# Reordered sums on VectorE and a full-width state decay in a retention plus maxout-FFN kernel

## The chip, the cores and the metric

The kernel runs on one core of one Trainium2 chip. The metric is the device time of one execution in microseconds. Four runs of the kernel before gave 776.54, 776.88, 778.55 and 776.59 us, a median of 776.73 us. The profile was taken on one execution, and its times are read with the clock of that execution; the granted TensorE clock was 1.00 over the whole span.

## The reference

```python
# q, k, v: (8, 8, 576, 64); x: 4608 tokens of 512
scores = scale * np.matmul(q, k.transpose(0, 1, 3, 2))
gamma = 1.0 - 2.0 ** (-5.0 - np.arange(H))
Dmat = np.where(rel >= 0, gamma ** rel, 0.0)          # rel = position of query - position of key
attn_out = np.matmul(scores * Dmat, v)
x = attn_out.transpose(0, 2, 1, 3).reshape(B * S, H * D)
h = np.maximum(np.maximum(x @ w1, x @ w2), x @ w3)    # 512 -> 768
out = h @ w_out                                       # 768 -> 512
```

The weights w1, w2, w3 and w_out arrive as float64 and are converted on the chip; everything is computed in float32.

## The kernel before

**Tiles and stages.** The 4608 tokens are 36 chunks of 128 (C) and 9 tiles of 512 (NT), numbered t = 0 to 8. Attention goes chunk by chunk with a running state: `scores` makes the products of queries and keys, `state` and `keep` carry the sum of keys times values to the next chunk, `values` makes the attention output, which is the FFN's input xT. `keep` multiplies a state by the decay over one chunk, gs, on VectorE (a chunk that starts a sequence, line 268) or on GpSimd (line 271). The FFN of tile t runs on TensorE (PE) while the attention of tile t + 1 is threaded into it: the last loop of the kernel alternates the steps that `steps(t + 1)` lists with `next(work)` on the generator `ffn(t)`. So the order on every engine is written out by hand; no scheduler moves anything.

**Plain and summed products.** A plain up product multiplies 512 tokens by one of w1, w2, w3 for one block of 128 hidden columns (`up_plain`, PE line 610); the first of the three is copied to h by ScalarE (line 615) and the other two are joined into h by a maximum on VectorE (line 614). Tile t = 0 does all its blocks in that way, and tile t = 1 the blocks fb = 2 and 3. Every other block uses `up`: a scheme with 20 smaller products in place of 24, whose factors are sums of pieces of x (X_SUMS) and of the weights (W_SUMS), and whose outputs are joined by VectorE additions and maxima (line 567, JOINS) after ScalarE copied them out of PSUM (line 572). The down product is plain for t = 0 (`downs_plain`, line 597) and a seven-product scheme after it (`downs`, line 427).

**The sums.** X_SUMS are 13 additions or subtractions of 128x256 on VectorE for each tile t > 0. W_SUMS are 19 such operations for each pair fp of hidden blocks, done once, in place where possible. All of them are issued by `combine`, line 346. They are queued in the list order: `weight_sums(0)` and `weight_sums(2)` at the start of tile t = 1, `weight_sums(1)` after its plain blocks. The sums for w_out (`sums_of_outs`, two on VectorE, lines 386 and 387, and two on GpSimd, lines 390 and 391, for each of three pairs) are queued while tile t = 0 does its down products.

**Who issues them and when.** `chore(n)` takes n entries from two queues, `urgent` first (attention work of VectorE that `soon` put off) and then `chores` (the sums). In tile t = 0 the down loop calls `chore(2)` after each of fb = 3, 4 and 5. In tile t = 1 each plain block has three steps, one for each of w1, w2, w3; a step issues its PE products and its copy or maximum, and after it `chore(8)` is called:

```python
for step, cost in enumerate(steps_of_one):
    if fb in plain:
        chore(8)
```

So the entries that `chore` issues after the step of w2 stand on VectorE's queue ahead of the maximum of w3.

**PSUM.** Plain and summed products share two pools of two banks each: ps_x (plain block 2, then chains A and B of the summed products) and ps_y (plain block 3, then chains E, C and D). A bank is handed out again when its last reader, a ScalarE copy or a VectorE operation, is done. After the plain block 3 of tile t = 1, chain E takes the bank that the maximum of w2 read, and chain C the one that the maximum of w3 reads.

**The start.** SyncE (SP) issues the loads: q, k and v of chunk 0 and of chunk 1, then the two loads of gs (line 692), then those of chunks 2 and 3 with the first weights between them. gs is 128 rows by 4 head pairs by 1 number; its source in HBM has 64 equal numbers for each head and row, of which one is read. The tile named fill only takes room.

Of the kernel before, what the change touches and what calls it, by code (L numbers as in the profile page):

```python
# [40 lines left out]
FP32 = mybir.dt.float32  # L41
# [4 lines left out]
ALU = mybir.AluOpType  # L46
# [4 lines left out]
NH = NT // 2  # L51
BY_PE = 7
AHEAD = 3
FILL = 192
PARTS = 20

X_SUMS = """s19 = a12 + a14, s15 = s19 - a22, s3 = a22 - a12, s10 = s3 - a13, s13 = a12 + a13, s20 = s10 + a23,
            s14 = a24 - s15, s11 = s20 + a24, s11 = a21 - s11, s7 = s11 - s13, s6 = s19 + s7,
            s16 = a11 - s11, s16 = s16 - a14"""
W_SUMS = """b33 = b13 + b33, n1 = b13 + b43, n2 = n1 - b41, n3 = b11 - n2, n4 = b33 - b32, b43 = b43 + n4,  # L60
            b23 = b43 - b23, b43 = b41 - b43, n5 = b22 + b23, b41 = b41 - n5, b21 = b21 - b41,
            b23 = b32 + b23, b22 = b22 - b21, b32 = b22 - b32, n6 = b31 + n2, n7 = b42 + n4,
            b42 = b42 - n5, b31 = b31 + b32, n8 = b12 - n4"""

PRODUCTS = """E a11 b12, E a14 b42, B s15 n5, A a22 b21, C s3 b23, B s19 b41, A s10 b32, C a13 b31, B s6 n2, A s13 b22,
              C a11 b11, B s14 n1, A s11 n4, D s7 b43, B a23 n6, A s20 b33, D s16 b13, B a21 n3, A a21 n8, A a24 n7"""
# [6 lines left out]
         "A7": [("A1", ("A1", "B6"), ALU.add), ("A1", ("A1", "A5"), ALU.max), ("hi", ("A1", "A7"), ALU.max)]}  # L73
X_SUMS, W_SUMS = ([x.split() for x in text.split(",")] for text in (X_SUMS, W_SUMS))
PRODUCTS = [x.split() for x in PRODUCTS.split(",")]
# [4 lines left out]
def kernel(  # L80
# [14 lines left out]
    nc = tc.nc  # L95
    P = 128
    B, H, S, D = q.shape
    N, DM = out.shape
    DF = moe_w1.shape[1]
    NP = H // 2  # L100
# [6 lines left out]
    const = ctx.enter_context(tc.tile_pool(name="const", bufs=1))  # L107
# [18 lines left out]

    gk = const.tile([C, H], FP32, name="gk")
    one, top, inf, first = (const.tile([P, 1], FP32, name=n) for n in ("one", "top", "inf", "first"))
    gs = const.tile([P, NP, 1], FP32, name="gs")
    const.tile([P, FILL // 4], FP32, name="fill")  # L130
    gq = const.tile([P, 2, NP // 2, C], FP32, name="gq")
    nc.scalar.dma_start(gk[:], key_decay)
    nc.vector.memset(one[:], 1.0)
    nc.scalar.copy(first[:], one[:])
# [15 lines left out]
    def start_of(g):  # L150
        r = -g * C % S
        return r if r < C else None
# [21 lines left out]
    def chore(n=1):  # L174
        for _ in range(n):
            if urgent or chores:
                (urgent or chores).popleft()()  # L177

    def soon(step):

        if spread:
            urgent.append(step)
        else:
            step()
# [63 lines left out]
    def begins(g):  # L248
        return g + 1 < NG and start_of(g + 1) != 0

    def half(j):
        return slice(D * j, D * (j + 1))
# [12 lines left out]
    def keep(g):  # L265
        def step(t, kv):
            if start_of(g) is not None:
                nc.vector.tensor_tensor(t[:], kv[:], gs[:].to_broadcast([P, NP, D]), op=ALU.mult)
            else:
                nc.vector.tensor_tensor(t[:], kv[:], states[g][:], op=ALU.add)  # L270
                nc.gpsimd.tensor_tensor(t[:], t[:], gs[:].to_broadcast([P, NP, D]), op=ALU.mult)

        if begins(g):
            t = states[g + 1] = stp.tile([P, NP, D], FP32, tag="state", name="state")
            soon(partial(step, t, kvs[g]))
# [46 lines left out]
    def output(chunks, o, t, i):  # L322
# [9 lines left out]
        if i == CPT - 1 and t > 0:  # L332
# [4 lines left out]
            def step(n, dst, _, a, sign, b):  # L337
                combine(*(xS[t][x] for x in (dst, a, b)), sign)
                if dst not in (later[0] for later in X_SUMS[n + 1:]):
                    made[t].add(dst)  # L340

            for n, line in enumerate(X_SUMS):
                soon(partial(step, n, *line))

    def combine(dst, a, b, sign):
        nc.vector.tensor_tensor(dst, a, b, op=ALU.add if sign == "+" else ALU.subtract)  # L346
# [191 lines left out]
    def weight_sums(fp):  # L538
# [3 lines left out]

        for dst, _, a, sign, b in W_SUMS:
            chores.append(partial(step, dst, a, sign, b))
        chores.append(partial(summed_fp.add, fp))

    def late_room():
        pool = late["pool"]
        late["W"] = [pool.tile([P, NF, P], FP32, name=f"n{n}") for n in range(1, 9)]
        late["X"] = {n: pool.tile([P, NH], FP32, name=n)[:] for n in sorted({x[0] for x in X_SUMS})}  # L550

    converting = convert_all()

    def convert(n):
        for _ in range(n):
            next(converting, None)
# [35 lines left out]
    def downs_plain(t, h):  # L592

        ps = [(ps_x, ps_y)[m % 2].tile([P, DM], FP32, tag="xy"[m % 2], name="down") for m in range(NT // P)]
        for fb in range(NF):
            for m, b in enumerate(ps):
                nc.tensor.matmul(b[:], lhsT=h[:, fb, m * P:(m + 1) * P], rhs=w_sb["out", fb],  # L597
                                 start=(fb == 0), stop=(fb == NF - 1))
                if fb == NF - 1:
                    osb = opool.tile([P, DM], FP32, tag="osb", name="osb")  # L600
                    nc.scalar.copy(osb[:], b[:])
                    nc.sync.dma_start(out[t * NT + m * P:t * NT + (m + 1) * P, :], osb[:])
            yield

    def up_plain(t, h, fb, i):
        ps = (ps_x, ps_y)[fb % 2].tile([P, NT], FP32, tag="xy"[fb % 2], name="up")
        first_of_all = t == 0 and (fb, i) == (0, 0)
        for cols in (slice(0, NT - C), slice(NT - C, NT)) if first_of_all else (slice(0, NT),):
            for dc in range(NDC):
                nc.tensor.matmul(ps[:, cols], lhsT=w_sb[i, fb][:, dc * P:(dc + 1) * P], rhs=xT[t][:, dc, cols],  # L610
                                 start=dc == 0 and cols.start == 0, stop=dc == NDC - 1,
                                 skip_group_check=first_of_all)
        if i > 0:
            return lambda: nc.vector.tensor_tensor(h[:, fb, :], h[:, fb, :], ps[:], op=ALU.max)
        return lambda: nc.scalar.copy(h[:, fb, :], ps[:])

    def ffn(t):

        h = hpool.tile([P, NF, NT], FP32, tag="h", name="h")
        if t == 0:  # L620
            for fp, i in units:
                for fb in (2 * fp, 2 * fp + 1):
                    maximum = up_plain(t, h, fb, i)
                    if CPT not in qks:
                        maximum()
                        transposes(CPT)
                        convert(4)
                        continue
                    convert(4)
                    maximum()  # L630
                yield
            convert(6)
            for fb, _ in enumerate(downs_plain(t, h)):
                convert(4 if fb < 2 else 4 * len(pieces))
                if fb == 2:
                    while_converting.close()
                    late["pool"] = ctx.enter_context(tc.tile_pool(name="late", bufs=1))
                    late_room()
                    sums_of_outs()
                elif fb > 2:  # L640
                    chore(2)
                if fb in (1, 3):
                    yield
            yield
            return
        if t == 1:
            spread.append(True)
            weight_sums(0)
            weight_sums(2)
        plain = (2, 3) if t == 1 else ()  # L650
        order = (2, 3, 0, 1, 4, 5) if t == 1 else (0, 1, 4, 5, 2, 3)
        total = sum(24 if fb in plain else len(PRODUCTS) for fb in order)
        count = parts = 0
        for n, fb in enumerate(order):
            if fb not in plain:
                while fb // 2 not in summed_fp:
                    chore()
            steps_of_one = up_plain_all(t, h, fb) if fb in plain else up(t, h, fb)
            for step, cost in enumerate(steps_of_one):
                if fb in plain:  # L660
                    chore(8)
                elif step % 2 or step % 5 == 4:
                    chore(len(urgent) > 0)
                elif step % 4 == 2 and chores:
                    chores.popleft()()
                count += cost or 1
                if count * (NF // 2 * 3) >= (parts + 1) * total:
                    parts += 1
                    yield
            if n % 2:  # L670
                sums_of_hidden(h, fb // 2)
                if fb in plain:
                    weight_sums(fb // 2)
        chore(len(urgent))
        for n, _ in enumerate(downs(t, h)):
            chore(4)
            if n in (1, 3):
                yield
        yield
# [8 lines left out]
    for g in range(CPT):  # L688
        load(g)
        if g == 1:  # L690
            for j in range(2):
                nc.sync.dma_start(gs[half(j)], state_decay[half(j), :, D * j:D * j + 1])
    load_weights(1)
    load(CPT)
    load_weights(4)
# [131 lines left out]
```

## Time and profile before

| what | value |
|---|---|
| median of 4 runs | 776.73 us |
| the profiled execution, its own time | 776.54 us |
| its span, first to last instruction | 774.8 us |
| PE busy | 766.9 us (99%) |
| VectorE (DVE) busy | 566.6 us (73%), 1249 instructions |
| ScalarE (ACT) busy | 326.1 us (42%) |
| GpSimd (POOL) busy | 99.2 us (13%) |
| DMA, first 20 us | 0.98 of 16 engines, 224 GB/s |
| DMA, 160 to 180 us | 0.39 of 16 engines, 74 GB/s |

The span lacks 1.74 us of the execution's own time; that part lies outside the instructions. A busy PE is not proof that it never waits, because the ends of pipelined matmuls are modelled; where it waits is read from the times at which matmuls start, and from the list of waits. Times "at 148.29" are microseconds from the start of the span. A timeline row gives start, duration, engine, line, operation, written and read tiles with their shape, the count, and in brackets idle time ahead of it and what ended it.

### The profile page before, as it was taken

Reading aid. Unit: us, or ns where it says so; the run is one execution under the profiler, and the core shown is the slowest. Engines: PE = TensorE matmul, PEld = TensorE weight load, DVE = VectorE, ACT = ScalarE, POOL = GpSimd, SP = SyncE. Lnnn points to the kernel's source line nnn. Section 1 sums busy time; section 2 is a strip of 40 time slices with the busy share of each in tenths; the row PEclk is TensorE's granted clock in tenths of the full one; section 3 lists DMA queues with packets and bytes.
Section 4 is the critical chain, followed back from the end, with each engine's and each line's share of the span. In section 5 each row is a group of like instructions: output and inputs, shape, how many; then the busy total and the mean of one; then the engine's idle time right before and its main releaser. Section 6 shows DMA issues by size and latency. Waiting matters only on the chain.

```text
span 774.8 us, 14508 instructions
## 1 busy us (share of the span) xinstructions
PE 766.9 (99%) x5032; PEld 626.5 (81%) x5032; DVE 566.6 (73%) x1249; ACT 326.1 (42%) x811; POOL 99.2 (13%) x124
## 2 busy tenths in 40 slices
PE   9899999999999999999999999999999999999998
PEld 7545454688888888888888888888888888888887
DVE  3998979899677857785769657875778567855672
ACT  3665631154154514452345234532544154514651
POOL 2110012111101201111111111110012001200000
PEclk9999999999999999999999999999999999999999
DMA  9995643333333332343233333333333324001001
GB/s 224 240 224 130 169 102 100 57 58 60 87 58 58 58 75 54 61 81 67 61 55 58 58 97 59 57 58 96 58 56 58 80 48 81 2 15 41 2 1 55
DMA packets 237082, 59.20 MB, mean 76 GB/s; under 512 B 217936, under 2 KB 235728, under 8 KB 237008
## 3 DMA queue, kind: packets, MB, share of 16 engines
q1 hardware_dynamic: 236432, 57.94, 34.8%
q8 instruction: 39, 0.64, 0.3%
q10 hardware_dynamic: 576, 0.33, 0.1%
q14 instruction: 35, 0.29, 0.1%
HBM read 48.76 MB, written 9.44 MB: 75 GB/s over the span
## 4 chain that ended last, share of the span: by engine, by line
PE 94%; DVE 4%; DMA 1%; issue 0%; ACT 0%; POOL 0%; DVEq 0%; POOLq 0%; ACTq 0%
PE a L587 18%; PE b L587 15%; PE dx L427 11%; PE up L610 8%; PE c L587 8%; PE dz L427 5%; PE d L587 5%; PE e L587 5%; PE s L242 4%; PE o L298 4%; PE dy L427 3%; PE down L597 2%; PE kv L262 2%; PE o L311 2%; DVE w L346 1%; DVE n L346 1%
## 5 line engine op out<-in xcount | busy, mean ns | idle before, releaser
L567 DVE TENSOR_TENSOR part<-part 128x256 f32<-128x256 f32 x460 | 207.1, 459 | 80.6 <-ACT part L572 72.9
L572 ACT COPY part<-b 128x256 f32<-128x256 f32 x230 | 85.7, 372 | 125.7 <-PE b L587 112.5
L572 ACT COPY part<-a 128x256 f32<-128x256 f32 x276 | 102.8, 373 | 84.9 <-PE a L587 74.0
L610 PE MATMUL up<-xT,w 128*128 128x512 f32 (+2 forms) x200 | 84.7, 578 | 1.5 <-DVE w L516 1.5
L587 PE MATMUL a<-s,w 128*128 128x256 f32 x276 | 82.3, 380 | 0.0
L213 POOL TENSOR_TENSOR vd<-vraw,gk 128x512 f32<-128x512 f32 x36 | 40.1, 1113 | 328.9 <-DMA vraw<-in_v_dram 228.4
L587 PE MATMUL b<-s,n 128*128 128x256 f32 x276 | 82.1, 379 | 0.0
L610 PEld LDWEIGHTS up<-xT,w 128*128 128x128 f32 x200 | 36.8, 190 | 43.6 <-issue 39.2
L587 PEld LDWEIGHTS b<-s,n 128*128 128x128 f32 x276 | 52.4, 190 | 7.1
L587 PEld LDWEIGHTS a<-s,w 128*128 128x128 f32 x276 | 52.3, 190 | 7.3 <-issue 0.2
L587 PE MATMUL c<-xT,w 128*128 128x256 f32 x184 | 56.0, 386 | 0.0
L587 PE MATMUL b<-xT,n 128*128 128x256 f32 x184 | 55.3, 382 | 0.0
L587 PE MATMUL d<-s,w 128*128 128x256 f32 x184 | 54.7, 379 | 0.0
L587 PE MATMUL a<-xT,n 128*128 128x256 f32 x184 | 47.2, 379 | 0.0
L587 PE MATMUL e<-xT,w 128*128 128x256 f32 x184 | 47.2, 379 | 0.0
L567 DVE TENSOR_TENSOR h<-part 128x256 f32<-128x256 f32 x92 | 41.8, 455 | 6.6
L427 PE MATMUL dx<-To,H 128*128 128x256 f32 (+1 forms) x204 | 44.9, 370 | 0.0
L434 ACT COPY part<-dx 128x256 f32<-128x256 f32 (+1 forms) x34 | 10.5, 362 | 80.1 <-PE dx L427 77.9
L177 DVE TENSOR_TENSOR xT<-o,gq 128x512 f32<-128x512 f32 x28 | 18.1, 686 | 33.9 <-PE o L311 33.9
L427 PEld LDWEIGHTS dx<-To,H 128*128 128x128 f32 x204 | 36.6, 190 | 5.5 <-issue 1.0
L242 PEld LDWEIGHTS s<-qT,kT 64*128 64x128 f32 x576 | 33.8, 188 | 7.9 <-PE b L587 4.0
L587 PEld LDWEIGHTS e<-xT,w 128*128 128x128 f32 x184 | 35.0, 190 | 5.2 <-issue 0.2
(104 smaller groups left out, 1283.0 us busy)
## 6 DMA issues: line engine op xcount, KB each, us to landing
bits<-in_moe_w_dram SPq DMA_DIRECT2D x36, 256.0 KB, 5.0
out_dram<-osb SPq DMA_DIRECT2D x35, 256.0 KB, 2.1
kraw<-in_k_dram SPq DMA_DIRECT2D x32, 256.0 KB, 2.9
vraw<-in_v_dram SPq DMA_DIRECT2D x32, 256.0 KB, 3.5
qraw<-in_q_dram SPq DMA_DIRECT2D x464, 16.0 KB, 1.8
kxraw<-in_k_dram SPq DMA_DIRECT2D x464, 16.0 KB, 1.8
bits<-in_moe_w_out_dram SPq DMA_DIRECT2D x6, 512.0 KB, 4.6
qraw<-in_q_dram SPq DMA_DIRECT2D x6, 256.0 KB, 4.4
```

What stands on the lines that cost most here:

```text
L177: (urgent or chores).popleft()()
L213: nc.gpsimd.tensor_tensor(t[:], raws.pop(("v", g))[:], gk[:].unsqueeze(2).to_broadcast([C, H, D]), op=ALU.mult)
L242: nc.tensor.matmul(s[j][:, p, :], lhsT=kT[r, p, :], rhs=qT[r, p, :], start=True, stop=True)
L262: nc.tensor.matmul(kvs[g][half(h % 2), h // 2, :], lhsT=kr[r:, h, :], rhs=vds[g][r:, h, :], start=True, stop=True)
L298: nc.tensor.matmul(o[n % 2][half(c), m, n // 2, :], lhsT=vds[g][:, h, :], rhs=sts[g][:, h % 2, h // 2, :], start=m == 0 and n < 2, stop=be ...
L311: nc.tensor.matmul(o[n % 2][half(c), m, n // 2, :old], lhsT=states[g][r, h // 2, :], rhs=qks[g]["q"][r, h // 2, :old], start=False, stop=True,
L346: nc.vector.tensor_tensor(dst, a, b, op=ALU.add if sign == "+" else ALU.subtract)
L427: nc.tensor.matmul(o, lhsT=hS[n](fp)[:, m * P:(m + 1) * P], rhs=late["T"][n][:, fp, cols], start=first and fp == 0 and (m == 0 or last and ...
L567: nc.vector.tensor_tensor(out, a, b, op=op)
L572: nc.scalar.copy(t[:], ps[step[0]][:])
L587: nc.tensor.matmul(ps[chain][:], lhsT=factor(w, fb), rhs=xS[t][x], start=n == 1, stop=ends, skip_group_check=True)
L610: nc.tensor.matmul(ps[:, cols], lhsT=w_sb[i, fb][:, dc * P:(dc + 1) * P], rhs=xT[t][:, dc, cols], start=dc == 0 and cols.start == 0, stop= ...
```

## The change

It does three things. It writes X_SUMS and W_SUMS in another order, with the same operations in them, so that a sum less often reads what the sum right ahead of it wrote. It changes how many entries `chore` takes at two places: after the down blocks fb = 3, 4 and 5 of tile t = 0 it takes 4, 0 and 2 in place of 2, 2 and 2, and after the step of w2 of the last plain block it takes 4 in place of 8. And gs becomes 128 rows by 4 head pairs by 64 numbers, loaded in full, and is read without repetition. The tile gs moves behind gq and fill grows from 192 to 224 bytes, so gq stays where it was and every later tile lies 1024 bytes further on.

```diff
-FILL = 192
+FILL = 224
-X_SUMS = """s19 = a12 + a14, s15 = s19 - a22, s3 = a22 - a12, s10 = s3 - a13, s13 = a12 + a13, s20 = s10 + a23,
-            s14 = a24 - s15, s11 = s20 + a24, s11 = a21 - s11, s7 = s11 - s13, s6 = s19 + s7,
-            s16 = a11 - s11, s16 = s16 - a14"""
-W_SUMS = """b33 = b13 + b33, n1 = b13 + b43, n2 = n1 - b41, n3 = b11 - n2, n4 = b33 - b32, b43 = b43 + n4,
-            b23 = b43 - b23, b43 = b41 - b43, n5 = b22 + b23, b41 = b41 - n5, b21 = b21 - b41,
-            b23 = b32 + b23, b22 = b22 - b21, b32 = b22 - b32, n6 = b31 + n2, n7 = b42 + n4,
-            b42 = b42 - n5, b31 = b31 + b32, n8 = b12 - n4"""
+X_SUMS = """s19 = a12 + a14, s3 = a22 - a12, s15 = s19 - a22, s10 = s3 - a13, s13 = a12 + a13, s20 = s10 + a23,
+            s14 = a24 - s15, s11 = s20 + a24, s11 = a21 - s11, s7 = s11 - s13, s16 = a11 - s11, s6 = s19 + s7,
+            s16 = s16 - a14"""
+W_SUMS = """b33 = b13 + b33, n1 = b13 + b43, n4 = b33 - b32, n2 = n1 - b41, b43 = b43 + n4, n3 = b11 - n2,
+            b23 = b43 - b23, n7 = b42 + n4, n5 = b22 + b23, b43 = b41 - b43, b41 = b41 - n5, b23 = b32 + b23,
+            b21 = b21 - b41, b42 = b42 - n5, b22 = b22 - b21, n6 = b31 + n2, b32 = b22 - b32, n8 = b12 - n4,
+            b31 = b31 + b32"""
...
-    gs = const.tile([P, NP, 1], FP32, name="gs")
     const.tile([P, FILL // 4], FP32, name="fill")
     gq = const.tile([P, 2, NP // 2, C], FP32, name="gq")
+    gs = const.tile([P, NP, D], FP32, name="gs")
...
-                nc.vector.tensor_tensor(t[:], kv[:], gs[:].to_broadcast([P, NP, D]), op=ALU.mult)
+                nc.vector.tensor_tensor(t[:], kv[:], gs[:], op=ALU.mult)
...
-                nc.gpsimd.tensor_tensor(t[:], t[:], gs[:].to_broadcast([P, NP, D]), op=ALU.mult)
+                nc.gpsimd.tensor_tensor(t[:], t[:], gs[:], op=ALU.mult)
...
-                    chore(2)
+                    chore({3: 4, 4: 0, 5: 2}[fb])
...
-                    chore(8)
+                    chore(4 if (fb, step) == (plain[-1], 1) else 8)
...
-                nc.sync.dma_start(gs[half(j)], state_decay[half(j), :, D * j:D * j + 1])
+                nc.sync.dma_start(gs[half(j)], state_decay[half(j), :, half(j)])
```

## The prediction

> **What bounds the kernel now.** I read the page first, then the list of waits of PE, then the timelines of PE and VectorE around the one wait found there, then the first 20 us.
>
> ```profile
> span 774.8 us, 14508 instructions
> ...
> PE 766.9 (99%) x5032; PEld 626.5 (81%) x5032; DVE 566.6 (73%) x1249; ACT 326.1 (42%) x811; POOL 99.2 (13%) x124
> ```
>
> PE sets the time. What a change can win is time in which PE waits. The list of PE's waits from 26 us to the end has a single row:
>
> ```profile
> PE c L587 <- DVE h L614: 1.2, 1, 1.2
> ```
>
> The change leaves PE's order untouched, so apart from the first 26 us this wait is all that there is to win. PE's timeline shows it:
>
> ```profile
> 138.99 7.13 PE L610 MATMUL up<-xT,w 128*128 128x512 f32 x16
> 145.96 1.03 PE L587 MATMUL e<-xT,w 128*128 128x256 f32 x4
> 146.82 0.59 PE L587 MATMUL b<-s,n 128*128 128x256 f32 x2
> 147.25 0.59 PE L587 MATMUL a<-xT,w 128*128 128x256 f32 x2
> 149.01 0.70 PE L587 MATMUL c<-s,w 128*128 128x256 f32 x2 [1.17 <-DVE h L614]
> ```
>
> Pairs start 0.43 us apart (146.82, 147.25), so c was due at 147.68 and started at 149.01: 1.33 us lost (the 1.17 counts from a modelled end). Chain C needs the ps_y bank that VectorE's last maximum of block 3 reads. VectorE's timeline tells why that was late:
>
> ```profile
> 129.52 0.42 DVE L346 TENSOR_TENSOR n<-n,w 128x256 f32<-128x256 f32 x1
> 129.98 0.42 DVE L346 TENSOR_TENSOR n<-w,n 128x256 f32<-128x256 f32 x1
> 130.32 0.42 DVE L346 TENSOR_TENSOR n<-w,w 128x256 f32<-128x256 f32 x1
> ...
> 143.98 1.28 DVE L177 TENSOR_TENSOR st<-s,causal 128x512 f32<-128x512 f32 x2
> 145.18 0.41 DVE L346 TENSOR_TENSOR w<-w,w 128x256 f32<-128x256 f32 x1
> 145.63 0.43 DVE L346 TENSOR_TENSOR w<-w 128x256 f32<-128x256 f32 x1
> 145.97 0.75 DVE L346 TENSOR_TENSOR n<-w,n 128x256 f32<-128x256 f32 x2
> 146.76 0.42 DVE L346 TENSOR_TENSOR w<-w,n 128x256 f32<-128x256 f32 x1
> 147.10 1.26 DVE L346 TENSOR_TENSOR w<-w,w 128x256 f32<-128x256 f32 x1
> 148.29 0.67 DVE L614 TENSOR_TENSOR h<-h,up 128x512 f32<-128x512 f32 x1
> ```
>
> Its product was ready when PE turned to e, at 145.96 plus some 0.15 of modelled tail. VectorE reached it at 148.29, behind six sums. Also visible: a sum that reads its predecessor's result starts 0.46 us after it (129.52 to 129.98), an independent one 0.34 (129.98 to 130.32). The sum at 147.10 took 1.26 in place of 0.42; GpSimd's vd ran from 146.80 for 1.28.
>
> **The change part by part.**
>
> *Fewer entries beside the last plain product but one.* `chore(8)` issued two masks and six sums ahead of the maximum; `chore(4)` issues the two masks and two sums. The six took 148.29 - 145.18 = 3.11 us, the first two 0.79, so the maximum moves up by 2.32 us, to 145.97. PE is not ready before about 146.12, so VectorE now waits for PE, and the bank is free at 146.12 + 0.67 = 146.8, 0.9 us ahead of 147.68. This edit alone removes the 1.33 us.
>
> *The order of the sums.* Up to that maximum, W_SUMS of fp = 0 and 2 have about eight and seven sums right behind their source; the new order keeps about one each. 13 gaps of 0.12 are 1.6 us. X_SUMS go from six to two: 0.5 us for each tile. On the path this adds margin to a wait that is gone; in tiles 2 to 8 no PE wait exists that X_SUMS could shorten. So 0 of its own. What covers it is VectorE's new waiting for PE.
>
> The Trainium skill, VectorE: DVE Perf Modes, section on the DRAIN you can't avoid, speaks against this edit: by its measurement a semaphore between chained operations costs nothing extra. The rows above disagree (0.46 against 0.34 us). By the rows the order saves 2 us of VectorE ahead of the maximum, by the page nothing; PE's gain would be 1.33 us by either.
>
> *Chore 4, 0, 2 in tile 0.* One pair of w_out sums (lines 386, 387) moves from between the transposes to ahead of xT, where VectorE idles 4.58 us before 116.31. The two pairs took 124.17 to 126.67, the second stretched to 1.74 us beside GpSimd's own subtractions; one pair alone is 0.76. So VectorE reaches W_SUMS 1.7 us sooner: more of the same margin. GpSimd's pair goes into its 10.12 us of idleness ahead of 123.12. It waits there for PE's down products of block 2, which are over by 112.8.
>
> *What is put off.* Four sums now stand behind the maximum. VectorE ended that row at 152.06 and idled 3.88 us to 155.94. Now its maximum ends 2.15 us sooner, four sums cost 1.34 to 1.82, and GpSimd's vd stretches a sum there (0.85) and not ahead of the maximum: it ends at 152.1 to 152.6. The next join, which follows PE, comes 1.33 sooner, at 154.6. Two us are left. Behind that VectorE is 96% busy (34.55 of 36 us from 156 to 192) and PE's margins are thin: E at 176.91 needs a bank that a join frees at 176.66, 0.25 us. As VectorE's stretch begins with work that PE releases, it moves up with PE; but GpSimd's vd at 164.37 waits for a load on SP's queue, which does not move up, so collisions fall elsewhere. Ends: 0 and 1.08 us (VectorE not moving up at all, 1.33 - 0.25). I take 0.1, nearer to 0, since the number of operations is the same.
>
> The Trainium skill, SBUF — State Buffer, section on who interferes with whom, has the rule behind the 1.26 us row: a VectorE operation with two SBUF inputs and a GpSimd operation that reads SBUF exclude each other. By it the maximum, which has one input in PSUM, is safe from that vd; by the row alone the block could strike it as well, but at 146.12 it starts ahead of the vd.
>
> *gs in full.* The two loads keep their place on SP's queue and their 512 pieces, each 256 bytes and not 4. The queue behind them ends in q of chunk 3, for which PE waits at 16.20, and from there st, expo, frac, mant and w on VectorE follow without a break to the first up product at 25.18. So a delay of that load goes into the span undiminished. The answer by stretch:
>
> ```profile
> 6.00:7.00 1.00, 1.00 (x7) 0.78 (x5) 0.00 (x0) 0.59 (x1) 0.99 (x1) 1.00 1.20 271
> 7.00:8.00 1.00, 1.00 (x16) 0.97 (x16) 0.00 (x0) 0.00 (x0) 0.06 (x1) 1.00 1.08 239
> 8.00:9.00 1.00, 1.00 (x12) 0.86 (x8) 0.73 (x2) 0.21 (x1) 0.00 (x0) 1.00 0.79 171
> 9.00:10.00 1.00, 1.00 (x26) 0.89 (x26) 0.56 (x1) 0.86 (x2) 0.72 (x1) 1.00 0.99 243
> ```
>
> The last two columns are DMA share and GB/s. 126 KB more at 271 GB/s are 0.47 us: the upper end. In the two slices in which gs moves the share falls to 0.79 and 0.99 from 1.20, so there is room of 0.6; filled, the cost is 0: the lower end. Less than nothing is excluded, as bytes are only added. I take 0.15, nearer to the room. Its reader at 10.27 already waits 0.7 us for gs; the state is used by PE only at 14.70.
>
> One of GpSimd's products with gs takes 0.61 us; the nearest with two full operands (line 391) 0.73. 24 times 0.12 lies on an engine 13% busy whose states PE nowhere waits for. The shift by 1024 bytes has no row; I take 0.
>
> **Sum.** 774.8 - 1.33 + 0.1 + 0.15 = 773.7 of span; with the 1.74 us around it 775.46, against 776.54. The median of the runs stands 0.19 above the profiled one, so 775.6.
>
> **The rivals.**
>
> *VectorE's backlog takes the gain back.* For it: 96% busy and 0.25 us of margin. Against it: equal work, released by PE. Price 0.5 to 1.08 us: 776.0 to 776.6.
>
> *The other side: the sums put off carry lateness into the saturated stretch.* If the two idle us ahead of 154.6 are not there (the vd later than at 146.80, the sums at the dependent pace), the four sums and the stretch, 2.7 us, arrive at 176.9 together with the 1.33: 2.7 + 1.33 - 0.25 = 3.8 us of PE waiting, 776.73 - 1.18 + 3.8 = 779.3. It decides once VectorE comes more than 2 us late to the join at 154.6; less is absorbed. Against it speaks the 3.88 us idle row.
>
> *The change doesn't do what it says:* the maximum stays late, through something ahead of it that I missed, and only gs remains: 776.73 + 0.15 to 0.47, 776.9 to 777.2. Against it: the 2.32 us are counted from rows.
>
> *gs dear:* gain in full, 0.47 paid: 775.9.
>
> *More than counted:* a start shorter by over 0.4 us, 775.0. No row speaks for it.
>
> **How the numbers follow.** My own forecast 0.55 (775.2 to 775.9, gs dear included), backlog 0.16, not done 0.08, the other side 0.07, more than counted 0.14. 0.2% of 776.73, about what a measurement of this kernel can tell from no change, is 1.55 us: faster means under 775.18, slower over 778.28. Faster 0.14, same 0.79, slower 0.07. The range leaves out the other side and the ends of the small cases: 774.9 to 777.0.
>
> **What would show it.** Right: no PE wait for L614 at about 147.7, c 0.43 us behind a, and VectorE idle for PE before both maxima of block 3; VectorE's first W sum at about 125.7 (127.89 before); first up product at 25.2 to 25.6 (25.18). Wrong: a new PE wait for a join (line 567) between 150 and 192, or PE's wait for q of chunk 3 longer by more than 0.5 us.

## The result, and the profile after

The changed kernel takes 775.62 us (median of 33 runs, 774.7 to 778.56). The kernel before, with 53 runs, is at 777.07 us (774.82 to 779.07). The ratio is 0.9984 with a 95% interval of 0.9979 to 0.9989: 1.45 us by the medians (the ratio is not the quotient of the two medians), just under 0.2%, and a gain, since the interval lies below 1. The profiled execution took 775.8 us with a span of 774.0 us, against 776.54 and 774.8.

The totals on the page of the kernel after:

```profile
span 774.0 us, 14511 instructions
...
PE 766.4 (99%) x5032; PEld 626.2 (81%) x5032; DVE 563.2 (73%) x1249; ACT 326.0 (42%) x811; POOL 101.9 (13%) x124
```

VectorE works 3.4 us less with as many instructions, GpSimd 2.7 us more with as many. The list of PE's waits, over the whole span, has nothing later than 26 us:

```profile
PE up L611 <- DVE w L517: 1.6, 1, 1.6
PE warm L148 <- POOL ident masks.py:199: 1.4, 1, 1.4
PE qt L232 <- DMA qraw<-in_q_dram: 1.2, 1, 1.2
PE kt L232 <- DMA kraw<-in_k_dram: 0.4, 1, 0.4
```

The wait for the last maximum of block 3 is gone. PE's timeline at the place where it was (line numbers are one higher than before):

```profile
139.17 7.13 PE L611 MATMUL up<-xT,w 128*128 128x512 f32 x16
146.14 1.03 PE L588 MATMUL e<-xT,w 128*128 128x256 f32 x4
147.00 0.59 PE L588 MATMUL b<-s,n 128*128 128x256 f32 x2
147.43 0.59 PE L588 MATMUL a<-xT,w 128*128 128x256 f32 x2
147.87 0.59 PE L588 MATMUL c<-s,w 128*128 128x256 f32 x2
```

c follows a by 0.44 us, the plain pace. VectorE's timeline shows what stands ahead of the maximum now:

```profile
125.87 0.39 DVE L347 TENSOR_TENSOR w<-w 128x256 f32<-128x256 f32 x1
...
142.98 0.69 DVE L615 TENSOR_TENSOR h<-h,up 128x512 f32<-128x512 f32 x1 [2.03 <-PE up L611]
143.58 1.28 DVE L178 TENSOR_TENSOR st<-s,causal 128x512 f32<-128x512 f32 x2
144.78 0.41 DVE L347 TENSOR_TENSOR w<-w 128x256 f32<-128x256 f32 x1
145.11 0.42 DVE L347 TENSOR_TENSOR w<-w,n 128x256 f32<-128x256 f32 x1
146.34 0.69 DVE L615 TENSOR_TENSOR h<-h,up 128x512 f32<-128x512 f32 x1 [0.81 <-PE up L611]
...
154.68 0.43 DVE L568 TENSOR_TENSOR part<-part 128x256 f32<-128x256 f32 x1 [3.44 <-ACT part L573]
```

Two masks and two sums after the maximum of w2, then 0.81 us of idleness for PE, then the maximum at 146.34. VectorE waits for PE and no longer PE for VectorE.

That gives 1.33 us, but the span fell by only 0.78. To find the rest, the start of each of PE's 5032 matmuls in the run after was set against the same matmul in the run before; where the difference changes, time is won or lost:

```
from            after - before, us
25.2            +0.18     first up product; the start was later
147.7 to 149    -1.15     the wait for L614 (1.33) is gone
149             -1.25     c's second matmul: 0.10 more
to 176          -1.22     0.04 given back
410.8           -1.11     d of tile 5
492.6           -1.00     d of tile 6
574.7           -0.90     d of tile 7
657.3           -0.78     d of tile 8, and so to the end
```

Two entries were in no term of the forecast's sum. When PE missed the bank in the kernel before, it also lost 0.10 us on restarting (its row for c has 0.70 in place of 0.59), so the wait's disappearance is worth 1.43. And in each of the last four tiles the run after loses 0.108 us at the first product of a chain D, 0.43 in all. The list of PE's waits shows none of the four. The list of its weight loads, from 150 us to the end, does, with a fifth at 176; the kernel before has neither row there:

```profile
PEld d L588 <- DVE part L568: 1.0, 4, 0.2
...
PEld e L588 <- DVE part L568: 0.2, 1, 0.2
```

PEld is the loading of a product's weights into TensorE, which runs beside the product before it.

### The profile page after: what moved, and what is told of

It is laid out like the page before. It is cut to its first block, busy times and chain, and to the rows that moved or that the text cites. A ratio compares the mean times of both kernels' runs of the same rounds, so it can differ in the third digit from the quotient of the medians.

```text
span 774.0 us, 14511 instructions
## 1 busy us (share of the span) xinstructions
PE 766.4 (99%) x5032; PEld 626.2 (81%) x5032; DVE 563.2 (73%) x1249; ACT 326.0 (42%) x811; POOL 101.9 (13%) x124
## 4 chain that ended last, share of the span: by engine, by line
PE 97%; SPq 1%; DVE 1%; DMA 1%; issue 0%; ACT 0%; DVEq 0%
PE a L588 18%; PE b L588 16%; PE dx L428 11%; PE up L611 11%; PE c L588 8%; PE dz L428 5%; PE d L588 5%; PE e L588 5%; PE s L243 4%; PE o L299 4%; PE down L598 3%; PE dy L428 3%; PE o L312 2%; PE kv L263 2%; SPq L210 1%; DMA qraw<-in_q_dram 1%
## 5 line engine op out<-in xcount | busy, mean ns | idle before, releaser
L272 POOL TENSOR_TENSOR state<-state,gs 128x256 f32<-128x256 f32 x24 | 18.4, 766 | 168.9 <-DVE state L271 168.9
```

The lines of the kernel that those rows point to most:

```text
L272: nc.gpsimd.tensor_tensor(t[:], t[:], gs[:], op=ALU.mult)
```

## The experiments

My theory after the result: the smaller `chore` alone frees PE, the order of the sums and the moved w_out sums only add margin behind it, and the wide gs costs what is missing. The rivals: the order, or the moved sums, would free PE alone; and the four late losses come from the sums put off. Each ratio is against runs of the kernel before that were taken beside it on the same chip.

### The smaller take alone

```diff
-                    chore(8)
+                    chore(4 if (fb, step) == (plain[-1], 1) else 8)
```

> Only the number of entries after the step of w2 of the last plain block is changed, from 8 to 4. My theory (the maximum of w3 is late because of what stands ahead of it on VectorE): PE's wait of 1.33 us for L614 is gone, chain C follows chain A after 0.43 us, and the median is 1.3 to 1.4 us under the kernel before (ratio 0.9982 to 0.9983). Rival (the order of the sums is what counts): a wait of 0.5 us or more is left. First up product within 0.3 us of 25.2, no PE wait after 150 us.

774.96 us (774.34 to 775.65, 6 runs) against 776.99 (23 runs): ratio 0.9969 (0.9957 to 0.9981). In its trace c starts 0.43 us behind a (148.22, 147.79), no wait for line 614 is listed, and none of the four late losses occurs. One edit of one line does all that the change wins. By the traces it does more: behind the first up product this execution lasts 748.2 us, that of the whole change 748.7. The times alone don't show that, as the two intervals overlap. The span, 773.9, is nearly that of the whole change only because in this execution the first up product started at 25.72, outside the 0.3 us around 25.2 that I had expected. The median lies 2.03 us lower, more than the 1.3 to 1.4 expected; the section on the prediction comes back to that.

### The order of the sums alone

```diff
-X_SUMS = """s19 = a12 + a14, s15 = s19 - a22, s3 = a22 - a12, ...
-W_SUMS = """b33 = b13 + b33, n1 = b13 + b43, n2 = n1 - b41, n3 = b11 - n2, ...
+X_SUMS = """s19 = a12 + a14, s3 = a22 - a12, s15 = s19 - a22, ...
+W_SUMS = """b33 = b13 + b33, n1 = b13 + b43, n4 = b33 - b32, n2 = n1 - b41, ...
```

> Only the two lists of sums are in the new order. The maximum of w2 of the last plain block cannot start before PE has finished its product (142.8 us on the clock of the kernel before, against 143.38 then), so at most 0.6 us of the 2 us that the order saves reach the maximum of w3; behind it come two masks and six sums, with or without a stretch by GpSimd's vd. My theory: PE's wait shrinks from 1.33 to between 0 and 0.6 us, and the median is 0.7 to 1.4 us lower. Rival (the saved 2 us all count, as an unclipped queue would have it): no wait at all and the maximum of w3 starts when PE is ready, at about 146.2. Second rival (a semaphore between chained operations costs nothing): VectorE's sums keep their times and the wait stays 1.33.

775.42 us (774.27 to 777.39, 9 runs): ratio 0.9981 (0.9971 to 0.9991). 0.50 us of the wait are left, inside the 0 to 0.6 expected; the median is 1.57 us lower, a little more than the 0.7 to 1.4 expected and than the 0.83 us that this trace shows, and the interval holds both. VectorE's timeline, and then PE's row for c:

```profile
142.92 0.69 DVE L614 TENSOR_TENSOR h<-h,up 128x512 f32<-128x512 f32 x1 [1.43 <-PE up L610]
...
146.39 1.27 DVE L346 TENSOR_TENSOR n<-w,n 128x256 f32<-128x256 f32 x1
...
147.59 0.67 DVE L614 TENSOR_TENSOR h<-h,up 128x512 f32<-128x512 f32 x1
```

```profile
148.31 0.70 PE L587 MATMUL c<-s,w 128*128 128x256 f32 x2 [0.34 <-DVE h L614]
```

The new order saves VectorE its time (four sums in that row start at 145.06, 145.39, 145.72 and 146.06, a pitch of 0.33 to 0.34 us), but most of what it saves ahead of 142.92 is lost again: there VectorE waits 1.43 us for PE's product of w2. That maximum starts only 0.46 us sooner than before (143.38), and 0.24 more are saved between it and the last one, which so comes 0.70 sooner (147.59 against 148.29); PE came to c 0.13 later by its own start, and 0.46 + 0.24 + 0.13 is the 0.83. All six sums still stand there, one of them stretched to 1.27 us beside GpSimd's vd.

### The moved w_out sums alone

```diff
-                    chore(2)
+                    chore({3: 4, 4: 0, 5: 2}[fb])
```

> Only the entries taken after the down blocks 3, 4 and 5 of tile 0 are changed, to 4, 0 and 2: VectorE begins its W sums some 1.7 us sooner. My theory (the maximum of w2, which waits for PE, clips what is saved ahead of it): that maximum starts at about 142.8 to 143.0, at most 0.6 us sooner than before, and six sums and GpSimd's vd still stand ahead of the maximum of w3. PE's wait is 0.7 to 1.3 us, the median 0 to 0.7 us lower (ratio 0.9991 to 1.0000). Rival (all that is saved ahead counts): no wait, ratio 0.9980.

776.23 us (774.55 to 778.9, 10 runs) against 777.34 (17 runs): ratio 0.9985 (0.9972 to 0.9999), more of a gain than I had expected, though the interval nearly touches 1. In the trace the wait is 1.17 us. The clip is the same:

```profile
143.11 0.69 DVE L614 TENSOR_TENSOR h<-h,up 128x512 f32<-128x512 f32 x1 [1.05 <-PE up L610]
```

VectorE comes early to block 3, waits 1.05 us for PE, and then issues the six sums at the old pace; two of them, at 146.49 and 147.58, take 1.16 and 0.94 us beside GpSimd's vd and H.

### The sums without gs, and gs without the sums

The first kernel is the whole change with gs narrow as before; the second is the kernel before with gs in full alone.

```diff
-                nc.gpsimd.tensor_tensor(t[:], t[:], gs[:], op=ALU.mult)
+                nc.gpsimd.tensor_tensor(t[:], t[:], gs[:].to_broadcast([P, NP, D]), op=ALU.mult)
...
-                nc.sync.dma_start(gs[half(j)], state_decay[half(j), :, half(j)])
+                nc.sync.dma_start(gs[half(j)], state_decay[half(j), :, D * j:D * j + 1])
```

> The changed kernel with gs loaded as one number again and read by repetition: the three edits on the sums alone. My theory: the whole 1.33 us and the 0.1 us of restart are won, and the four restarts of 0.11 us that the changed kernel shows in tiles 5 to 8 are gone, because GpSimd's product with gs takes 0.61 and not 0.73 us. First up product at 25.0 to 25.3. Time 1.4 us under the kernel before (ratio 0.9982) and some 0.6 us under the changed kernel. Rival (the restarts come with the earlier PE or the X order, not with gs): the four restarts stay, and the gain is 1.0 us.

> Only gs is changed: loaded in full and read without repetition. My theory: PE's wait of 1.33 us for L614 stays as it was; the first up product comes 0 to 0.4 us later; GpSimd's product with gs takes 0.73 and not 0.61 us, and with it four restarts of 0.11 us come in tiles 5 to 8. Together 0.4 to 0.8 us slower (ratio 1.0005 to 1.0010). Rival (gs costs nothing): same time, no restarts.

Without gs: 774.83 us (774.32 to 775.25, 6 runs), ratio 0.9967 (0.9956 to 0.9979); no wait for line 614, no late losses, a span of 773.5. With gs alone: 777.39 us (776.71 to 778.53, 11 runs), ratio 1.0003 (0.9995 to 1.0012). Its trace has the four late losses, at 413.0, 494.9, 577.0 and 659.6, 0.43 us in all (and 0.03 at 503.3), in a kernel in which no sum was moved. So the losses belong to gs, and the rival that put them down to the sums put off falls. The time alone would not have shown them: 0.40 us by the medians, and an interval that holds 1.

The wait for line 614 was 1.74 us in the run with gs alone, not 1.33. That asked whether gs lengthens it.

### The kernel before once more

> The kernel before, unchanged, for a second profile. My theory: its wait for L614 is not a fixed 1.33 us but depends on whether GpSimd's vd alone, or vd and the product with hidden sums behind it, lock out sums ahead of the maximum of w3 (one gives 1.2 to 1.4 us, both 1.6 to 1.8). Rival: 1.33 us again within 0.05. The first up product lies within 25.1 to 25.8 us, since the landing of the last q varies from execution to execution.

This is the kernel before, unchanged. 776.72 us, span 775.0, and a wait of 1.74 us too: gs has no part in it. The rows of its VectorE and its GpSimd say what the 0.41 us more are:

```profile
145.60 1.60 DVE L346 TENSOR_TENSOR n<-w,n 128x256 f32<-128x256 f32 x2
147.24 0.83 DVE L346 TENSOR_TENSOR w<-w,n 128x256 f32<-128x256 f32 x1
...
148.33 0.68 DVE L614 TENSOR_TENSOR h<-h,up 128x512 f32<-128x512 f32 x1
```

```profile
145.80 1.13 POOL L213 TENSOR_TENSOR vd<-vraw,gk 128x512 f32<-128x512 f32 x1 [16.95 <-DMA vraw<-in_v_dram]
146.89 0.90 POOL L404 TENSOR_TENSOR H<-h 128x256 f32<-128x256 f32 x1
```

vd is released by a load. In this execution it started at 145.80, where the run that the forecast used had it at 146.80; that is 1.52 us ahead of the time at which c was due, in place of 0.88. Both it and the H behind it now ran beside sums ahead of the maximum, two collisions in place of one. The size of the wait is thus not a constant of the kernel: it goes with the arrival of a load. The run with gs alone agrees: there vd came 1.54 us ahead, with the same wait of 1.74. The first up product started at 24.82, outside the 25.1 to 25.8 that I expected.

### gs loaded in full, but read with repetition

```diff
-                nc.gpsimd.tensor_tensor(t[:], t[:], gs[:], op=ALU.mult)
+                nc.gpsimd.tensor_tensor(t[:], t[:], gs[:, :, 0:1].to_broadcast([P, NP, D]), op=ALU.mult)
```

The product on VectorE (line 269) is edited in the same way; the rest is the kernel after, the full load included.

> The changed kernel with gs still loaded in full, but read as one number per head and row, by repetition. My theory (the four restarts of tiles 5 to 8 come from GpSimd's product with gs taking 0.73 and not 0.61 us, through VectorE's joins that it locks out): product back at 0.61 us, no restart after 154 us, some 0.43 us less than the changed kernel behind the same start; no PE wait for L614. Ratio to the kernel before 0.9967 to 0.9978. Rival (the load's bytes are what gs costs): restarts as in the changed kernel, ratio 0.9984 as it has.

774.91 us (774.56 to 776.38, 7 runs): ratio 0.9970 (0.9958 to 0.9982), against 0.9967 with the narrow load. No late losses. So the load costs nothing that these runs can show, nor does the shift of the later tiles by 1024 bytes, which this kernel keeps; the reading is what costs. The groups of GpSimd's product, of the kernel after and of this one (the figures are for 24 products: total, mean):

```profile
L272 POOL TENSOR_TENSOR state<-state,gs 128x256 f32<-128x256 f32 x24 | 18.4, 766 | 168.9 <-DVE state L271 168.9
L272 POOL TENSOR_TENSOR state<-state,gs 128x256 f32<-128x256 f32 x24 | 16.1, 669 | 166.8 <-DVE state L271 166.8
```

The kernel before, also with repetition, has 15.6 us and a mean of 651 ns for the same 24. The middle values are 732 ns in the kernel after, 622 in this one and 615 in the kernel before. How 0.12 us on an engine that is 13% busy reaches PE is seen in the first of the four places. The kernel before, timeline of VectorE, GpSimd and PE together:

```profile
408.23 1.17 DVE L567 TENSOR_TENSOR part<-part 128x256 f32<-128x256 f32 x2
408.39 0.72 POOL L271 TENSOR_TENSOR state<-state,gs 128x256 f32<-128x256 f32 x1 [8.67 <-DVE state L270]
...
411.12 0.39 DVE L567 TENSOR_TENSOR part<-e,part 128x256 f32<-128x256 f32 x1
...
411.68 0.59 PE L587 MATMUL d<-s,w 128*128 128x256 f32 x2
```

The kernel after, in the same way:

```profile
407.01 1.28 DVE L568 TENSOR_TENSOR part<-part 128x256 f32<-128x256 f32 x2
407.17 0.84 POOL L272 TENSOR_TENSOR state<-state,gs 128x256 f32<-128x256 f32 x1 [8.68 <-DVE state L271]
...
410.02 0.38 DVE L568 TENSOR_TENSOR part<-e,part 128x256 f32<-128x256 f32 x1
...
410.46 0.30 PEld L588 LDWEIGHTS d<-s,w 128*128 128x128 f32 x2 [0.24 <-DVE part L568]
410.46 0.70 PE L588 MATMUL d<-s,w 128*128 128x256 f32 x2
411.00 0.59 PE L588 MATMUL b<-xT,n 128*128 128x256 f32 x2
```

The same place in the kernel with gs in full but read with repetition:

```profile
406.33 1.18 DVE L568 TENSOR_TENSOR part<-part 128x256 f32<-128x256 f32 x2
406.49 0.73 POOL L272 TENSOR_TENSOR state<-state,gs 128x256 f32<-128x256 f32 x1 [8.37 <-DVE state L271]
...
409.24 0.39 DVE L568 TENSOR_TENSOR part<-e,part 128x256 f32<-128x256 f32 x1
...
409.78 0.60 PE L588 MATMUL d<-s,w 128*128 128x256 f32 x2
410.21 0.59 PE L588 MATMUL b<-xT,n 128*128 128x256 f32 x2
```

In the kernel after, GpSimd's product is 0.12 us longer, and the two joins that run beside it end as much later (1.28 in place of 1.17). VectorE goes on, with one gap of 0.10 us that all three traces have, to the join that reads e and gives its bank back. PE is 1.22 us ahead of the run before, that join only 1.10. d, due 0.43 us after its predecessor, comes on time but takes 0.70, and its successor follows 0.54 us behind it and not 0.43. The join ends at 410.40, 0.06 us ahead of d's start; before it ended at 411.51, 0.17 ahead. The weight load of d waited for that join and starts together with d, where it starts 0.12 us ahead of d in the kernel before (411.56) and 0.10 in the kernel with repetition (409.68).

The other three places are the same PE instruction of later tiles, and they look the same in every trace. In the eight executions that read gs with repetition, GpSimd's product takes 0.72 to 0.73 us there and the join gives the bank back 0.16 to 0.17 us ahead of d; in the three that read it in full, 0.83 to 0.84 us and 0.05 to 0.06. The eleven traces hold 506 products that begin a chain D. All 14 whose bank came back 0.05 to 0.06 us ahead lost 0.10 to 0.13 us, one at 0.13 us ahead lost 0.03, and none at 0.157 or more lost anything. The 0.05 to 0.06 us is also the time from the end of the late maximum to c in the kernel before (148.96 to 149.01), where c plainly waited; so d waited here too, although its start shows next to nothing of it. Two of the 14 have nothing to do with gs: near 165.4 us, in the second execution of the kernel before and in the run with the moved w_out sums alone, vd stretched a join to 1.08 us, and 0.13 us were lost. So the margin is what counts, and the longer read of gs is what takes it at the four places.

### Both again, side by side

> The three edits on the sums with gs loaded as one number, once more, on the same chip as the changed kernel. The spans so far are 748.2 us, plus the start of the first up product, plus PE's wait for L614 and 0.10 us of restart, plus later restarts. My theory: wait and restarts are 0, so the span is 748.2 plus the first up product, within 0.1; median 0.3 to 0.7 us under the changed kernel of the same call. Rival (the four restarts do not count in the median): the same median as the changed kernel within 0.2 us.

> The changed kernel, unchanged, beside the run without full gs. My theory: no wait for L614, four restarts of 0.11 us in tiles 5 to 8, span 748.2 + 0.43 plus the first up product; ratio to the kernel before 0.9975 to 0.9986. Rival: the restarts were an accident of one execution and are fewer or more.

The sums without gs: 775.04 us (774.08 to 775.64, 7 runs), ratio 0.9973 (0.9962 to 0.9984). The whole change: 775.67 us (775.04 to 777.22, 11 runs), ratio 0.9983 (0.9974 to 0.9992). The difference is 0.63 us. The two intervals overlap, but these runs were taken side by side: of the 77 pairs of one run of each, the sums without gs are the faster in 69. And every kernel in which the wait is gone and gs is read with repetition lies at 774.83 to 775.04, and the whole change lay at 775.62 and 775.67. The traces agree: the whole change again has its four losses (0.106 to 0.109 us each), the other has none.

A version without the wide read is thus the best one here, ahead of the kernel before and of the change. Among the three of that kind (the smaller take alone, all the sums, all with the full load) the runs can't choose.

## Why the prediction was right or wrong

**Right: the wait and the edit that ends it.** "This edit alone removes the 1.33 us" held: the smaller take alone wins as much as everything. The marks named for it are there: c 0.44 us behind a, VectorE idle for PE 2.03 and 0.81 us ahead of both maxima of block 3, the first W sum at 125.87 (forecast about 125.7), the first up product at 25.36 (25.2 to 25.6), and no new wait for a join after 150. The rivals "not done" and "the other side" are excluded by the same rows: VectorE ended the row after the maximum at 151.24 (150.83 plus 0.41), even before the 152.1 that I had forecast, and 3.44 us were idle ahead of the next join. vd came at 145.99 and stretched no sum there; the product behind it, H, stretched one, to 0.95. That the row is so much shorter than forecast was not worked out.

**Right, within the whole change: the order and the moved sums at 0.** With the smaller take in place they add nothing that can be measured (774.96 without them, 774.83 and 775.04 with them). What I hadn't worked out is their worth alone: 0.83 of 1.33 us for the order and 0.16 for the moved sums by one trace each, clipped where VectorE waits for the product of w2.

The pace behind that, 0.46 us for a sum that reads its predecessor's result against 0.34, stood up: in the new order sums follow at 0.33 to 0.34 us, and VectorE is busy 561.3 to 564.7 us in the six traces that have it, 566.2 to 568.7 in the five that don't. Ahead of the maximum the sums with the longer distance fall from 15 or 16 to 2, as counted in the forecast. The Trainium skill, VectorE: DVE Perf Modes, section on the DRAIN you can't avoid, has it from a test with eight copies that the semaphore between chained operations costs nothing extra; the rows of this kernel say 0.12 us for each sum that reads its predecessor's result, and the measurement decides. Whether the semaphore or the result itself is what the later sum waits for, no run here shows.

**Not needed, the backlog, 0.1 taken:** at the place named, E at about 176, PE lost 0.04 us in the first run after and 0.08 in the second; where gs is read with repetition it lost none, though the same sums were put off. So the term by itself measured 0, and the 0.04 to 0.08 came with the read of gs; that they are near 0.1 is luck. The rival with 0.5 to 1.08 us didn't come about.

**Not confirmed, the load of gs:** "So a delay of that load goes into the span undiminished", taken at 0.15. The full load with reads by repetition (0.9970) stands level with the narrow load (0.9967). The chain behind it doesn't pass delay on undiminished: in the run after, q of chunk 3 was taken 0.69 us later than before (16.89 against 16.20), and the first up product came 0.18 later. That product started anywhere from 24.72 to 25.81 in the eleven executions profiled, 25.26 on average in the four with the full load and 25.30 in the seven with the narrow one. Beside this scatter the load can't be seen, and 0.15 us could not have been: no run shows the term, and none excludes it. What was wrong is "undiminished".

**Wrong, the read of gs:** the step of the prediction that failed is that the 24 times 0.12 us "lies on an engine 13% busy whose states PE nowhere waits for", costed at 0. PE indeed never waits for a state. But that product holds up VectorE's joins, and a chain of joins with next to no break hands it to a bank for which PE had only 0.17 us of margin: 0.43 us in four places. The Trainium skill, SBUF — State Buffer, section on who interferes with whom, states the exclusion, and I had cited it for vd alone; I should have asked it of the lengthened instruction as well. On the maximum that section was right: the maximum at 146.34 ran beside the vd of 145.99 to 147.03 and took 0.69 us, not stretched.

**Mis-sized, the gain:** 1.33 was read from one execution. The restart adds 0.10, and the wait was 1.74 us in the second execution of the kernel before. So the whole change is worth, by these traces, 1.43 - 0.43 - 0.04 = 0.96 to 1.84 - 0.43 - 0.04 = 1.37 us of PE's time; the medians say 1.45. The four kernels that lose the wait and read gs with repetition lie 2.03 to 2.43 us under the kernel before by their medians, against the 1.43 to 1.84 of these traces; the intervals reach down to 1.2 to 1.6 us and so hold the 1.84, and nothing here explains the rest. The forecast took 1.08 off a median of four runs that lay 0.34 below that of 53. The two errors, a baseline too low and a gain too small, nearly cancel, and with them the load and the read of gs: 775.6 against 775.62 is closer than the working deserves.

The account as a whole: span = 748.2 + start of the first up product + wait for line 614 + the restarts. For the kernel before it is 748.2 + 25.18 + 1.33 + 0.10 = 774.8, for the kernel after 748.2 + 25.36 + 0.43 + 0.04 = 774.0, as measured; for each of the other nine runs the 748.2 comes out within 0.06 us, if small losses (0.13 us near 165.4 in two of them, 0.03 at 503.3 in the one with gs alone) are counted.

## What to carry to other kernels

Where an engine is 99% busy, find its one wait and then what is queued ahead of the operation that ends it: taking four entries out of that queue removed the whole wait, where reordering all of them removed 0.83 of 1.33 us. Savings ahead of an operation that then itself waits for the bound engine are clipped there, so ask of each saved microsecond whether it lies before or after that operation. And a longer instruction on an idle engine isn't free when it shuts out a saturated one: look at who shares its access, and at the margin of the next bank. Read the waits of the weight loads beside those of the products: in the trace after they named the five losses that the other list left out.

## What the runs showed of the hardware that I had not expected

- A PE product that just misses its bank costs 0.10 to 0.13 us, even where the list of PE's waits shows none: pair durations of 0.70 in place of 0.59, and 0.54 us to the next start in place of 0.43. A product that waits for its bank starts 0.05 to 0.06 us after the bank's last reader ends; a bank given back 0.16 us ahead was in time.
- GpSimd's product of 128x256 f32 takes 0.73 us with two full operands and 0.61 to 0.62 us where one of them repeats one number per head and row (24 instructions each, middle values).
- Reading 64 equal numbers in place of one for each head and row, about 126 KB more in the first 12 us, had no cost that shows (0.9970 against 0.9967), while the start of the first up product moves by 1.1 us from execution to execution.
